# GpSimd stores odd partitions of dV and dK of pair 0, SyncE the even ones; dV of pair 3 in one store

## The chip, the cores and the metric

The kernel runs on one core of one Trainium2 chip. The metric is device time in microseconds (us) of one execution of the whole program. The core has five engines with instruction queues of their own: TensorE (PE), VectorE (DVE), ScalarE (ACT), GpSimd (POOL) and SyncE (SP), and sixteen DMA engines that move data between HBM and the on-chip memory (SBUF, 128 partitions). A store or load ("a DMA") is issued by one of the queues, cut into packets, and shared among the DMA engines; when all of them are done, a semaphore tells it.

## The reference

Attention with one query per head, forward and backward: 32 heads, 8192 keys and values per head, 128 numbers each, all in bf16.

```python
B, H, Sq, Skv, Dh = 1, 32, 1, 8192, 128
scores = jnp.einsum('bhqd,bhkd->bhqk', q, k) * Dh ** -0.5
attn = softmax(scores)
out = jnp.einsum('bhqk,bhkd->bhqd', attn, v)
# and the gradients of out with respect to q, k, v for a given grad_out
```

The outputs are out, dq, dk and dv. K and V (67 MB each) are read, dK and dV (67 MB each) are written. Each row of dV is the row's attention weight times grad_out, and each row of dK is the row's score gradient times q: outer products.

## The kernel before

**Pairs.** The 32 heads are taken as 16 pairs. Keys and values of one pair are 16384 rows of 128 numbers. A tile holds them as [128 partitions, 128 rows, 128 numbers]: a partition has 128 consecutive rows, 32 KB, and a tile is 4 MB. `rows_of(x, j)` gives the same arrangement in HBM.

**Buffers.** There are three buffers for K and two for V. The gradients are written in place: `outer(j, which, r)` overwrites an eighth of the K or V tile of pair j with an eighth of dK or dV, by one product on the DVE (line 291). When it has done the last piece of a store, the store is issued (lines 296 to 306). A K buffer can be loaded again when the dK that stood in it has been stored, so the K load of pair 3 waits for the stores of dK of pair 0, and the V load of pair 2 for the stores of dV of pair 0.

**Order.** The order of instructions is written out by hand. For each pair: scores from K on the PE, after DVE transposes; softmax; the products with V; dV (eight pieces); then, in the next pair's turn, dK (eight pieces). For pairs 0 and 1 dK is made in one stretch before the next pair's scores. `load_v(j + 1)` is issued after dK of pair j - 1, `load_k(j + 2)` after dV of pair j. SyncE issues nearly all loads and stores, in program order, and waits at each for what it overwrites or needs. `ENDS` says after which eighths a store is issued: by default two halves for pairs under `SPLIT` = 4, one whole store after that, and other pieces for the last pair.

**Pair 0.** dV of pair 0 has a way of its own (lines 296 to 301). Its first half (64 of each partition's 128 rows, 16 KB a partition, 2 MB together) is stored by GpSimd as soon as four of the eight products are done; its second half by SyncE after the eighth. dK of pair 0 goes by the default, two halves from SyncE.

**How GpSimd's bytes are dealt out.** A store that SyncE issues for 128 partitions puts the same bytes on all sixteen DMA engines. For a store that GpSimd issues for n partitions the kernel's arithmetic takes it that k engines are used, k being the largest divisor of n up to 16, starting at a place that moves on by k with every request; `cursor` keeps count of that place. `turn_to(engine)` moves it on to a wanted engine with a tiny load of a few bytes into a tile that nothing reads (`turned`); `share_out` then stores the partitions `first`, `first + 3`, `first + 6`, ... of one entry of `SHARES`. So each entry `(engine, first, n)` says on which engines n partitions go: for example n = 39 goes to 13 engines, three partitions on each. The seven entries together are all 128 partitions, in unequal parts: engine 4 gets none, engines 0, 1, 2 and 15 get twelve each. With `max_dma_last_dim=8192` a partition's 16 KB go as two packets of 8 KB.

**Waits of GpSimd.** The requests of GpSimd take turns among eight semaphores, so each waits until the request eight before it has landed.

Of the kernel before, what the change touches and what calls it, by code (L numbers as in the profile page):

```python
# [11 lines left out]
BF16 = mybir.dt.bfloat16  # L12
# [2 lines left out]

XK_BUFS = 3
EARLY = 3
ENDS = {("dk", 15): (2, 4, 8), ("dv", 15): (4, 8)}
SPLIT = 4
CH = 16  # L20
TB = 4
# [3 lines left out]
QD = 32  # L25
LOADS = {("k", 0): 4, ("v", 0): 4, ("v", 1): 4, ("k", 2): 2}
SHARED = 64
SHARES = ((5, 2, 7), (6, 0, 39), (6, 1, 39), (15, 23, 25), (10, 98, 10), (5, 117, 4), (5, 118, 4))
GP = 4


# [1 line left out]
def kernel(  # L33
# [11 lines left out]
    nc = tc.nc  # L45
    P = 128
# [14 lines left out]
    consts = ctx.enter_context(tc.tile_pool(name="consts", bufs=1))  # L61
# [14 lines left out]
    def rows_of(x, j, c=0, parts=1):  # L76
        L = NT // parts
        return x[0, 2 * j:2 * j + 2].rearrange("b s d -> (b s) d").rearrange("(p n) d -> p n d", p=P)[:, c * L:(c + 1) * L, :]

    def slots(X, c, parts):  # L80
        L = NT // parts
        return X[:, c * L:(c + 1) * L, :]
# [19 lines left out]
    load_v(1)  # L102
    load_k(2)

    turned = consts.tile([17, len(SHARES), 2, 2], BF16)
    cursor = [0, 0]

    def turn_to(engine):
        n = (engine - cursor[0]) % 16
        if n:  # L110
            rows = n if n > 1 else 17
            nc.gpsimd.dma_start(turned[0:rows, cursor[1]],
                                k[0, 0].rearrange("(p n) d -> p n d", p=P)[0:rows, 0:2, 0:2])
            cursor[1] += 1
        cursor[0] = engine

    def share_out(dst, src):
        for engine, first, n in SHARES:
            turn_to(engine)
            last = first + 3 * n - 2  # L120
            nc.gpsimd.dma_start(dst[first:last:3], src[first:last:3], max_dma_last_dim=8192)
            cursor[0] = (cursor[0] + max(i for i in range(1, 17) if n % i == 0)) % 16

    ident = consts.tile([P, P], BF16)
# [162 lines left out]
    def outer(j, which, r):  # L287
        x = st[j]
        G, dst = (Kt[j], out_2) if which == "dk" else (Vt[j], out_3)
        rep, row = x["ds"] if which == "dk" else x["p"], qd[j][:, 0 if which == "dk" else 1, :]  # L290
        nc.vector.tensor_tensor(  # L291
            slots(G, r, NU).rearrange("p n (a b) -> p n a b", b=R),
            slots(rep, r, NU).unsqueeze(2).to_broadcast([P, CH, D // R, R]),
            row.rearrange("p (a b) -> p a b", b=R).unsqueeze(1).to_broadcast([P, CH, D // R, R]),
            op=ALU.mult)
        if (which, j) == ("dv", 0):
            if (r + 1) * CH == SHARED:
                share_out(rows_of(dst, 0)[:, 0:SHARED, :], G[:, 0:SHARED, :])
            elif r == NU - 1:
                nc.sync.dma_start(rows_of(dst, 0)[:, SHARED:NT, :], G[:, SHARED:NT, :])  # L300
            return
        ends = ENDS.get((which, j), (4, 8) if j < SPLIT else (8,))
        if r + 1 in ends:
            i = ends.index(r + 1)
            a, b = (ends[i - 1] if i else 0) * CH, (r + 1) * CH
            nc.sync.dma_start(rows_of(dst, j)[:, a:b, :], G[:, a:b, :])
# [49 lines left out]
    for j in range(HP + 1):  # L356
# [30 lines left out]
        if j == 0:  # L387
            blocks(1)
            first = psT.tile([P, 512], F32, tag="T", name="first")
# [9 lines left out]
        if ends and j > 0:  # L399
            gather_copy(p_, "ds")  # L400
            if early:
                half(j, 0)
            for r in range(NU):
                if j == HP and r == NU - 2:
                    result(o_all, out_0)
                    gather(p_, "ds", st[p_]["m"])
                    result(dq_all, out_1)
                outer(p_, "dk", r)
            if j + 1 < HP:
                load_v(j + 1)  # L410
# [7 lines left out]
        if not ends:  # L418
            gather_copy(p_, "ds")
            outer(p_, "dk", 0)  # L420
            outer(p_, "dk", 1)
# [104 lines left out]
```

## Time and profile before

| what | value |
|---|---|
| time, median of 3 runs | 632.86 us (632.41 to 633.36) |
| time of the profiled execution | 633.73 us |
| its span, first to last instruction | 631.9 us |
| bytes moved by DMA | 268.98 MB, 426 GB/s on average |
| SyncE's queue, GpSimd's queue (share of 16 engines) | 98.5%, 0.8% |
| GpSimd's stores of dV of pair 0: first and last issue | 31.06 us, 46.70 us |
| their median time from issue to landing, by size | 6.7 to 19.9 us |
| SyncE issues the second half of dV of pair 0 | 37.67 us |
| SyncE issues dK of pair 0, two halves | from 47.25 us |
| V load of pair 2, K load of pair 3 issued | 65.57 us, 77.33 us |
| SyncE issues the last store (half of dK of pair 15) | 621.92 us |

The page cuts the span into 40 slices of 15.8 us. Its DMA row gives the mean busy share of the sixteen DMA engines in tenths (9 is 90% or more). "q1 hardware_dynamic" is SyncE's queue, "q0 software_dynamic" GpSimd's, "q8 instruction" fetches instructions. In the list of issues, SPq and POOL are SyncE and GpSimd; the first number is the start in us, the second how long the issue took, and brackets give the time the engine had waited before, and for what. Line numbers are those of the kernel before; in the changed kernel the same lines stand three to four lower.

### The profile page before, as it was taken

What the parts mean: (1) busy time and instruction counts of PE and PEld (TensorE: products, weight loads), DVE (VectorE), ACT (ScalarE), POOL (GpSimd) and SP (SyncE); (2) the same over time, 40 slices, a digit from 0 to 9 for tenths busy, and PEclk for the clock granted to TensorE, in tenths of its full rate; (3) what the DMA queues carried; (4) which work ended last, traced back from release to release, by engine and by line L of the source; (5) the groups of instructions that cost most, each with busy time, mean ns of one, the idle gap of its engine ahead of it and who ended that gap; (6) DMA issues with size and microseconds to landing.
All of it is one profiled execution on the core that took longest, in us unless ns stands there. A gap on an engine that the chain in (4) does not pass through costs nothing.

```text
span 631.9 us, 8032 instructions
## 1 busy us (share of the span) xinstructions
PE 470.0 (74%) x3256; PEld 250.0 (40%) x3256; DVE 517.0 (82%) x654; ACT 205.4 (32%) x460; POOL 11.6 (2%) x23
## 2 busy tenths in 40 slices
PE   4787868878787877776887767857679876797671
PEld 1443444254443525334363432624436343252440
DVE  6589897989879898796978969879697986988873
ACT  2441434043341605234052330603415133160331
POOL 2040000000000000000000000000000000000000
PEclk9989787778798887779878798877887778887685
DMA  8999999999999999999999999999999999999997
GB/s 363 435 399 425 437 432 422 430 433 436 431 429 435 433 430 430 430 434 431 430 429 432 431 432 430 430 425 432 432 430 432 431 432 429 431 431 435 427 421 324
DMA packets 13140, 268.98 MB, mean 426 GB/s; under 512 B 2096, under 2 KB 2096, under 8 KB 2096
## 3 DMA queue, kind: packets, MB, share of 16 engines
q1 hardware_dynamic: 12192, 266.36, 98.5%
q0 software_dynamic: 816, 2.10, 0.8%
q8 instruction: 25, 0.41, 0.2%
q14 instruction: 11, 0.09, 0.0%
q10 hardware_dynamic: 96, 0.02, 0.0%
HBM read 134.23 MB, written 134.23 MB: 425 GB/s over the span
## 4 chain that ended last, share of the span: by engine, by line
DMA 54%; PE 30%; DVE 11%; ACT 3%; issue 1%; DVEq 0%; SPq 0%; ACTq 0%
DMA Vt<-in_v_dram 22%; DMA out_dram<-Vt 14%; PE T_ps L216 12%; DMA Kt<-in_k_dram 10%; PE s_ps L199 9%; DMA out_dram<-Kt 8%; DVE Kt L291 3%; PE acc_p L266 3%; DVE Vt L291 2%; DVE XK_sb L189 2%; PE acc_ds L266 2%; ACT XV_sb L221 2%; PE dp_ps L233 2%; PE m_ps L283 1%; DVE sT L206 1%
## 5 line engine op out<-in xcount | busy, mean ns | idle before, releaser
L199 PE MATMUL s_ps<-XK_sb,q_win 128*128 128x512 bf16 x512 | 156.7, 445 | 58.2 <-DVE XK_sb L189 53.6
L291 DVE TENSOR_TENSOR Vt<-p_rep,qd 128x2048 bf16<-128x2048 bf16 x128 | 154.5, 1223 | 43.2 <-PE acc_p L266 32.9
L189 DVE STREAM_TRANSPOSE XK_sb<-Kt 128x1024 f32<-128x1024 f32 x128 | 150.4, 1218 | 33.3 <-DMA Kt<-in_k_dram 29.5
L216 PE MATMUL T_ps<-ident_f,Vt 128*128 128x128 f32 x1024 | 171.0, 321 | 8.6 <-DMA Vt<-in_v_dram 8.6
L221 ACT COPY XV_sb<-T_ps 128x512 f32<-128x512 f32 x256 | 140.3, 589 | 90.9 <-PE T_ps L216 90.2
L216 PEld LDWEIGHTS T_ps<-ident_f,Vt 128*128 128x128 f32 x1024 | 136.8, 165 | 47.0 <-issue 23.7
L291 DVE TENSOR_TENSOR Kt<-ds_rep,qd 128x2048 bf16<-128x2048 bf16 x128 | 149.5, 1214 | 3.0 <-PE acc_ds L266 2.5
L199 PEld LDWEIGHTS <-q_win 128*128 128x128 bf16 x512 | 52.5, 112 | 149.2 <-issue 119.0
L266 PE MATMUL acc_p<-Vt,win 128*32 128x512 bf16 x512 | 57.7, 455 | 3.2 <-ACT win L256 3.2
L441 ACT ACTIVATE e<-sT,nbias 128x128 f32<-128x128 f32 x16 | 8.2, 516 | 149.1 <-DVE nbias L437 149.1
L266 PEld LDWEIGHTS <-win 128*32 128x32 bf16 x1024 | 22.8, 99 | 61.3 <-issue 49.9
L266 PE MATMUL acc_ds<-Kt,win 128*32 128x512 bf16 x512 | 41.2, 415 | 4.6 <-ACT win L256 4.6
L233 PE MATMUL dp_ps<-XV_sb,do_win 128*32 128x512 bf16 x512 | 34.1, 382 | 13.4 <-ACT XV_sb L221 13.4
L256 ACT COPY win<-ds 64x128 bf16<-64x128 bf16 x32 | 9.5, 296 | 99.1 <-DVE ds L328 98.9
L233 PEld LDWEIGHTS <-do_win 128*32 128x32 bf16 x512 | 14.3, 94 | 29.0 <-issue 22.4
L442 PE MATMUL m_ps<-rs,ones_f 128*128 128x1 f32 x32 | 7.5, 305 | 24.4 <-ACT e L441 24.4
L428 PE MATMUL m_ps<-ident_f,top 128*128 128x128 f32 x16 | 4.8, 300 | 23.5 <-DVE top L426 23.5
L206 DVE STREAM_TRANSPOSE sT<-s_ps 128x512 f32<-128x512 f32 x16 | 11.5, 717 | 12.6 <-PE s_ps L199 12.6
L442 PEld LDWEIGHTS m_ps<-rs,ones_f 128*128 128x128 f32 x32 | 6.2, 241 | 27.6 <-ACT e L441 27.6
L453 ACT ACTIVATE p_rep<-e,rinv 128x512 bf16<-128x512 f32 x16 | 11.5, 722 | 13.3 <-DVE rinv L451 13.3
L428 PEld LDWEIGHTS m_ps<-ident_f,top 128*128 128x128 f32 x16 | 2.1, 133 | 31.0 <-issue 25.4
L185 ACT COPY do_win<-do_cols 64x4 bf16<-64x4 bf16 x32 | 6.6, 206 | 16.1 <-PE dp_ps L233 15.8
(59 smaller groups left out, 155.6 us busy)
## 6 DMA issues: line engine op xcount, KB each, us to landing
Kt<-in_k_dram SPq DMA_DIRECT2D x14, 4096.0 KB, 29.0
Vt<-in_v_dram SPq DMA_DIRECT2D x14, 4096.0 KB, 29.0
out_dram<-Vt SPq DMA_DIRECT2D x11, 4096.0 KB, 31.9
out_dram<-Kt SPq DMA_DIRECT2D x11, 4096.0 KB, 24.7
out_dram<-Vt SPq DMA_DIRECT2D x9, 2048.0 KB, 21.5
out_dram<-Kt SPq DMA_DIRECT2D x9, 2048.0 KB, 20.1
Vt<-in_v_dram SPq DMA_DIRECT2D x8, 1024.0 KB, 22.9
Kt<-in_k_dram SPq DMA_DIRECT2D x4, 1024.0 KB, 8.1
```

Of the source, the lines that this page charges most:

```text
L189: nc.vector.transpose(XK[j, u][:].rearrange("p g w i -> p (g w i)"), slots(Kt[j], u, NU).rearrange("p g d -> p (g d)").bitcast(F32))
L199: nc.tensor.matmul(st[j]["s"][:], lhsT=q_win[:, c, at:at + P], rhs=cols[:, c // 2, c % 2], start=(u == 0 and c == 0), stop=(u == NU - 1 an ...
L206: nc.vector.transpose(sT[:].rearrange("p g r -> p (g r)"), x["s"][:])
L216: nc.tensor.transpose(T_ps[:, i, :], words[:, m * P:(m + 1) * P], ident_f[:])
L221: nc.scalar.copy(XV[j][:, b * TB:(b + 1) * TB, :], st[j].pop(("T", c))[:])
L233: nc.tensor.matmul(out[b * QD:(b + 1) * QD, :], lhsT=do_win[:, b // 2, e2, at:at + QD], rhs=cols[:, z, e2, :, b * QD:(b + 1) * QD], start= ...
L256: nc.scalar.copy(win[t * M:(t + 1) * M, :, at:at + 4], src[t * M:(t + 1) * M])
L266: nc.tensor.matmul(acc[which][b * QD:(b + 1) * QD, :], lhsT=win[:, g, at:at + QD], rhs=X[:, 4 * g:4 * g + 4, :].rearrange("p n d -> p (n d)"),
L291: nc.vector.tensor_tensor(slots(G, r, NU).rearrange("p n (a b) -> p n a b", b=R), slots(rep, r, NU).unsqueeze(2).to_broadcast([P, CH, D // ...
L441: nc.scalar.activation(e[:].rearrange("p (u g) -> p u g", u=NU), x["sn"], ACT.Exp, bias=nbias[:], scale=scale, accum_out=rs[:])
L442: nc.tensor.matmul(x["m"][:, 0:1], lhsT=ones_f[:], rhs=rs[:], start=True, stop=True, skip_group_check=True)
L453: nc.scalar.activation(x["p"][:], e[:].unsqueeze(2).to_broadcast([P, NT, R]), ACT.Copy, scale=rinv[:])
```

## The change

Three things.

- The first half of dK of pair 0 now goes the way of the first half of dV: `share_out` is called for both.
- In both, GpSimd stores the odd partitions only, in six pieces each, by two new lists; the pieces take every fourth partition instead of every third. SyncE stores the even partitions, in one store of 64 partitions, 1 MB. The second halves are stored by SyncE whole, as dV's was.
- dV of pair 3 is stored whole after its eighth product instead of in two halves.

GpSimd thus issues twelve stores instead of seven, and twelve turning loads instead of seven; its bytes stay at 2.10 MB.

```diff
-ENDS = {("dk", 15): (2, 4, 8), ("dv", 15): (4, 8)}
+ENDS = {("dk", 15): (2, 4, 8), ("dv", 15): (4, 8), ("dv", 3): (8,)}
-SHARES = ((5, 2, 7), (6, 0, 39), (6, 1, 39), (15, 23, 25), (10, 98, 10), (5, 117, 4), (5, 118, 4))
+SHARES = {
+    "dv": ((5, 15, 4), (6, 25, 26), (15, 31, 25), (6, 3, 3), (7, 1, 2), (5, 9, 4)),
+    "dk": ((0, 119, 3), (5, 23, 14), (7, 25, 26), (7, 79, 10), (5, 1, 6), (7, 3, 5)),
+}
-    turned = consts.tile([17, len(SHARES), 2, 2], BF16)
+    turned = consts.tile([17, len(SHARES["dv"] + SHARES["dk"]), 2, 2], BF16)
-    def share_out(dst, src):
-        for engine, first, n in SHARES:
+    def share_out(which, dst, src):
+        for engine, first, n in SHARES[which]:
             turn_to(engine)
-            last = first + 3 * n - 2
-            nc.gpsimd.dma_start(dst[first:last:3], src[first:last:3], max_dma_last_dim=8192)
+            last = first + 4 * n - 3
+            nc.gpsimd.dma_start(dst[first:last:4], src[first:last:4], max_dma_last_dim=8192)
             cursor[0] = (cursor[0] + max(i for i in range(1, 17) if n % i == 0)) % 16
-        if (which, j) == ("dv", 0):
+        if j == 0:
             if (r + 1) * CH == SHARED:
-                share_out(rows_of(dst, 0)[:, 0:SHARED, :], G[:, 0:SHARED, :])
+                share_out(which, rows_of(dst, 0)[:, 0:SHARED, :], G[:, 0:SHARED, :])
+                nc.sync.dma_start(rows_of(dst, 0)[0:P:2, 0:SHARED, :], G[0:P:2, 0:SHARED, :])
             elif r == NU - 1:
                 nc.sync.dma_start(rows_of(dst, 0)[:, SHARED:NT, :], G[:, SHARED:NT, :])
             return
```

## The prediction

> **What bounds the kernel now.** I read the page first, parts 2 and 3: is any resource full over the whole span?
>
> ```profile
> span 631.9 us, 8032 instructions
> PE 470.0 (74%) x3256; PEld 250.0 (40%) x3256; DVE 517.0 (82%) x654; ACT 205.4 (32%) x460; POOL 11.6 (2%) x23
> ...
> DMA  8999999999999999999999999999999999999997
> ...
> q1 hardware_dynamic: 12192, 266.36, 98.5%
> q0 software_dynamic: 816, 2.10, 0.8%
> ```
>
> The 16 DMA engines are full from the first slice to the last: SyncE's queue (q1) and GpSimd's (q0) take 99.3% of them. No compute engine passes 82%. The bytes don't change, so the time can move only by what a DMA engine loses (waiting, slowed packets) and by how unevenly the 16 finish. Second view, the stretches around the end and around GpSimd's burst (columns: stretch, its length, busy us of PE, PEld, DVE, ACT, POOL, clock, DMA share, GB/s):
>
> ```profile
> 626.00:627.50 1.50, 0.00 (x0) 0.00 (x0) 0.00 (x0) 0.00 (x0) 0.00 (x0) 0.50 0.92 393
> 627.50:628.50 1.00, 0.00 (x0) 0.00 (x0) 0.00 (x0) 0.00 (x0) 0.00 (x0) 0.50 0.58 246
> 628.50:629.50 1.00, 0.00 (x0) 0.00 (x0) 0.00 (x0) 0.00 (x0) 0.00 (x0) 0.50 0.19 82
> 629.50:630.50 1.00, 0.00 (x0) 0.00 (x0) 0.00 (x0) 0.00 (x0) 0.00 (x0) 0.50 0.04 16
> ...
> 32.00:38.00 6.00, 5.42 (x56) 3.34 (x56) 5.26 (x5) 4.07 (x9) 3.81 (x7) 1.00 1.00 362
> 38.00:46.00 8.00, 5.50 (x43) 2.23 (x43) 6.41 (x13) 0.87 (x4) 2.72 (x4) 0.79 1.02 426
> ```
>
> From 627.5 the engines drop out one by one; the last one works alone near 630.5. That tail is what another division of GpSimd's bytes can change. In 32 to 38 us, while GpSimd's first requests start, every engine is slowed: 362 GB/s against 426. Third view, the times at which SyncE and GpSimd issue:
>
> ```profile
> 65.57 0.34 SPq L94 DMA_DIRECT2D Vt<-in_v_dram  x1
> 72.29 4.87 SPq L306 DMA_DIRECT2D out_dram<-Vt  x2
> 77.33 0.49 SPq L88 DMA_DIRECT2D Kt<-in_k_dram  x1
> 85.41 4.87 SPq L306 DMA_DIRECT2D out_dram<-Kt  x2
> ...
> 38.03 0.56 POOL L121 DMA_DIRECT2D out_dram<-Vt  x1 [2.23 <-DMA out_dram<-Vt]
> 42.42 0.60 POOL L121 DMA_DIRECT2D out_dram<-Vt  x1 [2.75 <-DMA out_dram<-Vt]
> 46.70 0.59 POOL L121 DMA_DIRECT2D out_dram<-Vt  x1 [3.07 <-DMA out_dram<-Vt]
> ```
>
> GpSimd is already held by landings: each request waits for the one eight back. The V load of pair 2 leaves at 65.57 because it overwrites the V of pair 0.
>
> **The sixteen engines.** The trace's DMA packets carry start, duration and size but no engine. On one engine a packet starts 3 to 4 ns before the one ahead of it ends, so they can be chained into 16. The 8 KB packets of GpSimd on each chain come out at 24 four times, 18 three times, 16 twice, 14 four times, 12, 6 and 0 (two chains are confused by one packet): just what the arithmetic of `turn_to` and `share_out` gives to engines (0,1,2,15), (6,7,8), (10,11), (9,12,13,14), 3, 5 and 4. So I can name engines, and count the new lists the same way. One row is 16 KB, two packets of 0.306 us. Rows by engine, and the end of its last packet in us:
>
> - 0, 1, 15: 12 rows, now 12, 11, 11; ends 627.7 to 628.0
> - 2: 12, now 11; 629.44
> - 3: 6, now 7; 628.28. 5: 3, now 4; 627.76
> - 4: 0, now 0; 629.28
> - 6: 9, now 7; 630.67. 7 and 8: 9, now 12; 627.7
> - 9: 7, now 8; 629.64. 10: 8, now 8; 628.83
> - 11: 8, now 7; 628.92. 12, 13, 14: 7, now 6; 628.2 to 628.6
>
> Two things explain ends that don't follow the rows. Engine 4 is slow by itself: its 32 KB packets take up to 1.29 us instead of 1.213, some 8.8 us over the run, so it needs the lead that its missing rows give. And the 16 KB instruction fetches (25 on the page's q8, about 0.95 us, and some 0.5 us more of slowed data) go in turn to eight engines: those with 14, 16, 16, 14, 14, 14 and 6 packets (9 to 14, then 5) and one of 6, 7, 8, which is the one that ends last. I take it for engine 6, the next after 5.
>
> **The change, part by part.**
>
> *Rows moved.* Engine 6 loses two: 630.67 - 2 x 0.61 = 629.46. Engines 7 and 8 gain three: 627.7 + 1.83 = 629.5; they had stood idle 0.8 us for the last store (issued 621.92), so perhaps 628.7. Engine 9 gains one: 630.25. Engine 2: 628.83; the others stay below 629.
>
> *Even partitions on SyncE.* For dV and for dK 64 rows, 4 on each engine, 2.43 us each. GpSimd's 2.10 MB stay 2.10 MB. SyncE issues a 1 MB store of dV at about 31.1 and loses 1 MB of dK at 47.25, so its queue is the same up to the end of dK of pair 0, but the second half of dV now stands 2.43 us further back. It landed last at 64.61, on an engine that had 24 packets of GpSimd before it (7.3 us). Now that engine has had 14 for dV and perhaps 4 of dK by then (5.5 us): 2.43 - 1.83 = 0.6 later at least, 2.4 if it has had 24 again. Following the two rings packet by packet, one of GpSimd's for each of SyncE's, I get 1.6. The V load of pair 2 would thus leave at 67.2 instead of 65.57. Queued behind it on SyncE is the first store of dV of pair 1, at 72.29, which isn't reached; who waits is engine 4, first to run out. Its first packet of that load took 2.03 us where 1.21 is usual, so it already lost 0.81; it arrives no later than before, and each us of delay is lost to it. Engine 4: 629.28 + 1.6 = 630.9 (629.9 to 631.7).
>
> *GpSimd's longer chain.* Twelve stores and twelve turning requests instead of seven and seven. The six of dK start at 47.25, when the DVE has done the first half, and pass through two rounds of waiting for the request eight back. Before, such a request landed 17.3 to 20.3 us after issue; the same walk through the rings puts the last landing at 77 to 83. The K load of pair 3, which overwrites K of pair 0, now waits for it; it left at 77.33. It costs nothing while it leaves before about 87: the engines still have the stores of dV of pair 1, which engine 4 ended at 87.6 and the mean engine at 92.1, and the lead that a load needs was 2.4 us (65.57 to 69.17 less one packet). Behind it on SyncE stands a store at 85.41. If that cover is gone, engine 4 pays each us in full.
>
> A lag can add to this: GpSimd's first packets came 3.8 us after the issue at 31.06, while the DVE's products of line 291 ran (from 32.36), and the same products run from 42.59 to 51.76, over the first dK requests. If each of the two rounds lags so, the last landing is near 87, which is why rival 1 below gets more than a tenth. The Trainium skill's page "DMA: Bandwidth & Descriptors", section "SWDGE vs HWDGE vs iDMA", says as much against this place: GpSimd writes its descriptors into SBUF, and the DVE's two-port mode locks it out meanwhile. By that rule the K load leaves at 87 and the time is rival 1's lower end; without it, the walk's 77 to 83 and my sum stand.
>
> *The burst.* At 362 instead of 428 GB/s (2 to 30 us), the 6 us lost 0.93 us on every engine. The four first stores held 110 rows; now 58. If the loss follows rows it falls by 0.44; if it follows requests, by nothing; a second burst with dK could at most repeat it (+0.93), but single requests at 38 to 47 us ran at 426. I take -0.2. Ten more requests of some three tiny packets (6 ns each) add up to 0.2. Together nothing.
>
> *dV of pair 3 whole.* The first half was issued at 140.84; at 147.8 SyncE's queue still held the V load that landed at 161.7, so a whole store is not late, and the V load behind it waits for the second half's end in both. Cover gone, it would cost a store's lead, 2.4 us. One completion less: nothing.
>
> **Sum.** The last packet of the profiled execution was engine 6's at 630.67 (span 631.9, time 633.73). After: engine 4 at 630.9, +0.2. But this execution is 0.87 above the median 632.86, and engine 6 met one packet at 392.9 us that took 0.63 too long; without it the last would have been at 630.0, and the change +0.9. I take +0.65: **633.5 us**. The wait at engine 6 goes; engine 4, and 9 behind it, are late next.
>
> **The rivals.**
> 1. *The dK chain holds the K load* (the side of slower). If the dK requests land 25 us after issue, since V's 32 KB packets double each turn of the ring, the last comes near 90, the load leaves at 90.5 instead of 77.33, and engine 4 loses 3.5 us more: 632.86 + 0.65 + 3.5 = 637; at 88.5 it is 635. It decides from 87. For it: GpSimd's waits above; against: the walk. 22%.
> 2. *The V load isn't later*, or engine 4 gets its wait back. Then engine 9 (630.25, less up to 0.44) is last against 630.67, and engines 6, 7, 8 at 629.5: 0.4 to 1.5 gained, 631.5. 22%.
> 3. *The late engine isn't 6 but 7 or 8.* It gains three rows: 632.5, +1.8, 634.7. Against: the order of the fetches. 8%.
>
> **How the numbers follow.** My own case has 45%, from 632.4 to 634.4 by its bounds (engine 4's 629.9 to 631.7, the executions' own 0.5). Something unseen: 3%, slower. 0.2%, 1.27 us, is about what a measurement of this kernel can tell from no change. Faster than 631.6: 0.15 of rival 2 and 0.03 of mine, 0.18. Within: 0.33 of mine and 0.07 of rival 2, 0.40. Slower than 634.1: 0.09 of mine, 0.22, 0.08, 0.03: 0.42. The range, 631.2 to 635.6, leaves out the far ends of rivals 1 and 2, some 0.2.
>
> **What would show it.** The V load of pair 2 at 66.2 to 68 us (right), at 65.6 or earlier (rival 2); the K load of pair 3 at 77.3 to 84 (right), past 87 (rival 1); six GpSimd stores from line 124 before 43 us, six from 47; the DMA share between 628.5 and 630.5 still over 0.1 on average, and 32 to 38 us at 360 to 400 GB/s. I am wrong if the tail ends before 629.5 or the engines run empty after 77 us.

## The result, and the profile after

The changed kernel takes **637.13 us** (median of 6 runs, 636.52 to 638.32); the kernel before, beside it, 633.0 us (6 runs, 632.41 to 634.14). The ratio is 1.0063, with a 95% interval of 1.0052 to 1.0074: slower by 0.6%, 4.1 us. The forecast was 633.5 us, with a range of 631.2 to 635.6.

The profiled execution of the changed kernel took 636.52 us, 0.6 us below its median, where that of the kernel before was 0.7 us above its own. So the two traces lie only 2.8 us apart, and the other 1.3 us is between executions of one kernel.

The page of the changed kernel, parts 2 and 3:

```profile
span 634.8 us, 8048 instructions
...
DMA  8999999999999999999999999999999999999997
GB/s 362 433 403 420 394 417 426 430 435 435 435 422 440 429 429 430 433 434 428 433 436 431 426 425 435 433 427 428 431 430 426 436 428 431 434 431 433 430 417 316
...
q1 hardware_dynamic: 12064, 266.36, 98.3%
q0 software_dynamic: 1152, 2.10, 0.9%
```

The DMA engines are as full as before. The loss isn't idle time: the fifth and sixth slices of 15.8 us (63 to 95 us) show 394 and 417 GB/s, where every later one up to the last two is at 422 to 440. The engines are busy and move less. The same in stretches (columns as in the prediction), first the changed kernel:

```profile
32.00:38.00 6.00, 4.57 (x50) 2.71 (x48) 5.61 (x6) 3.63 (x8) 3.73 (x7) 1.00 0.98 373
...
62.00:70.00 8.00, 5.86 (x42) 2.61 (x40) 6.80 (x10) 4.60 (x11) 0.00 (x0) 0.62 1.03 411
70.00:78.00 8.00, 7.12 (x54) 3.94 (x54) 7.34 (x13) 2.57 (x7) 0.00 (x0) 0.95 1.02 379
78.00:86.00 8.00, 1.91 (x32) 0.77 (x32) 7.21 (x9) 0.59 (x2) 0.00 (x0) 0.90 0.95 387
86.00:100.00 14.00, 11.35 (x68) 7.88 (x68) 9.45 (x10) 4.40 (x8) 0.00 (x0) 0.81 1.01 434
62.00:86.00 24.00, 14.89 (x127) 7.32 (x124) 21.36 (x30) 7.75 (x19) 0.00 (x0) 0.83 1.00 392
```

and the kernel before:

```profile
62.00:70.00 8.00, 5.42 (x41) 3.05 (x41) 6.80 (x11) 4.02 (x10) 0.00 (x0) 0.74 1.03 435
70.00:78.00 8.00, 7.61 (x57) 4.11 (x56) 7.90 (x11) 3.25 (x7) 0.00 (x0) 0.83 1.04 446
78.00:86.00 8.00, 3.53 (x46) 2.18 (x45) 6.38 (x9) 0.81 (x3) 0.00 (x0) 1.00 0.95 408
...
62.00:86.00 24.00, 16.55 (x140) 9.34 (x141) 21.07 (x30) 8.07 (x20) 0.00 (x0) 0.86 1.01 430
```

From 62 to 86 us the sixteen engines move 392 GB/s instead of 430, with the DMA share at 1.00. Over 24 us that is 24 x (1 - 392/430) = 2.1 us of work. From 86 us on both kernels run at full rate.

The packet records say which packets are slow. I add up what packets of 8, 16 and 32 KB took beyond their usual 0.309, 0.611 and 1.213 us, as a mean per engine. Between 62 and 90 us that is 0.12 us before and **2.00 us** after; over the whole run it is 3.89 and 5.80 us, so nearly all of the difference is made there. Of the 2.00 us, 1.34 belong to the eight 32 KB packets of each engine that load V of pair 2, above all those at its beginning (up to 1.47 us too long) and towards its end; the rest to the stores just before. The slow packets come at the same times on many engines (74 to 77.6 us and 80.3 to 84.3 us), and go on after the last 8 KB packet of GpSimd has ended at 70.8 us.

The loss is paid at the end. The tail of the changed kernel:

```profile
627.50:628.50 1.00, 0.00 (x0) 0.00 (x0) 0.00 (x0) 0.00 (x0) 0.00 (x0) 0.50 1.06 452
628.50:629.50 1.00, 0.00 (x0) 0.00 (x0) 0.00 (x0) 0.00 (x0) 0.00 (x0) 0.50 1.08 460
629.50:630.50 1.00, 0.00 (x0) 0.00 (x0) 0.00 (x0) 0.00 (x0) 0.00 (x0) 0.50 0.58 246
630.50:631.50 1.00, 0.00 (x0) 0.00 (x0) 0.00 (x0) 0.00 (x0) 0.00 (x0) 0.50 0.35 147
631.50:632.50 1.00, 0.00 (x0) 0.00 (x0) 0.00 (x0) 0.00 (x0) 0.00 (x0) 0.50 0.12 49
632.50:633.50 1.00, 0.00 (x0) 0.00 (x0) 0.00 (x0) 0.00 (x0) 0.00 (x0) 0.50 0.08 33
```

From 628.5 to 629.5 us all engines still work (DMA share 1.08), where before the share was 0.19. The mean engine ends at 630.98 instead of 628.57 us, the last at 633.52 instead of 630.67. The mean engine is already 2.2 us late at the end of the V load of pair 3 (its sixteen landings come at 123.61 instead of 121.46 us in the mean), so what comes later adds next to nothing. The issues of SyncE and GpSimd:

```profile
67.72 0.34 SPq L97 DMA_DIRECT2D Vt<-in_v_dram  x1
71.39 4.87 SPq L310 DMA_DIRECT2D out_dram<-Vt  x2
76.56 0.34 SPq L91 DMA_DIRECT2D Kt<-in_k_dram  x1
...
40.10 0.80 POOL L124 DMA_DIRECT2D out_dram<-Vt  x1 [1.85 <-DMA out_dram<-Vt]
...
46.63 0.57 POOL L124 DMA_DIRECT2D out_dram<-Kt  x1 [5.16 <-DVE Kt L294]
...
59.16 0.56 POOL L124 DMA_DIRECT2D out_dram<-Kt  x1 [1.31 <-DMA out_dram<-Kt]
```

The V load of pair 2 leaves at 67.72 us (before 65.57), the K load of pair 3 at 76.56 us, not held by GpSimd's dK, whose last store had landed at 72.75 us.

### The profile page after: what moved, and what is told of

Its sections match the earlier page's. It is cut to its first block, busy times and chain, and to the rows that moved or that the text cites. A ratio compares the mean times of both kernels' runs of the same rounds, so it can differ in the third digit from the quotient of the medians.

```text
span 634.8 us, 8048 instructions
## 1 busy us (share of the span) xinstructions
PE 459.4 (72%) x3256; PEld 246.7 (39%) x3256; DVE 516.3 (81%) x654; ACT 205.9 (32%) x460; POOL 17.0 (3%) x33
## 4 chain that ended last, share of the span: by engine, by line
DMA 57%; PE 24%; DVE 12%; ACT 3%; issue 2%; DVEq 0%; ACTq 0%; SPq 0%
DMA Vt<-in_v_dram 35%; DMA out_dram<-Vt 21%; PE T_ps L219 14%; PE s_ps L202 4%; PE acc_p L269 4%; DVE Kt L294 3%; DVE XK_sb L192 3%; DVE Vt L294 3%; ACT XV_sb L224 2%; PE dp_ps L236 2%; PE acc_ds L269 1%; DMA Kt<-in_k_dram 1%; ACT win L259 1%; DVE sT L209 1%; ACT p_rep L457 0%
## 5 line engine op out<-in xcount | busy, mean ns | idle before, releaser
L202 PE MATMUL s_ps<-XK_sb,q_win 128*128 128x512 bf16 x512 | 152.0, 433 | 66.3 <-DVE XK_sb L192 61.5
L219 PE MATMUL T_ps<-ident_f,Vt 128*128 128x128 f32 x1024 | 169.0, 319 | 13.0 <-DMA Vt<-in_v_dram 13.0
L219 PEld LDWEIGHTS T_ps<-ident_f,Vt 128*128 128x128 f32 x1024 | 135.4, 164 | 49.9 <-issue 24.2
L269 PE MATMUL acc_p<-Vt,win 128*32 128x512 bf16 x512 | 55.9, 439 | 3.4 <-ACT win L259 3.4
L322 PEld LDWEIGHTS m_ps<-pd,ones_f 128*128 128x128 f32 x32 | 8.7, 285 | 8.2 <-DVE prod L252 7.2
```

The source lines that it names most:

```text
L202: nc.tensor.matmul(st[j]["s"][:], lhsT=q_win[:, c, at:at + P], rhs=cols[:, c // 2, c % 2], start=(u == 0 and c == 0), stop=(u == NU - 1 an ...
L219: nc.tensor.transpose(T_ps[:, i, :], words[:, m * P:(m + 1) * P], ident_f[:])
L269: nc.tensor.matmul(acc[which][b * QD:(b + 1) * QD, :], lhsT=win[:, g, at:at + QD], rhs=X[:, 4 * g:4 * g + 4, :].rearrange("p n d -> p (n d)"),
L322: nc.tensor.matmul(x["m"][:, 1:3], lhsT=ones_f[:], rhs=x["pd"][:], start=True, stop=True, skip_group_check=True)
```

## The experiments

Each run is compared with the kernel before on the same chip. "The stretch" below is 62 to 86 us; a run has either 427 to 433 GB/s there and at most 0.41 us of slow packets, or 363 to 409 GB/s and 1.2 to 3.8 us. The table gathers what the following paragraphs find; "dK's first half" counts the store transfers in which it leaves, by SyncE and by GpSimd.

| run | dK's first half: SyncE + GpSimd | stretch, GB/s | slow packets 62 to 90, us per engine | ratio to before |
|---|---|---|---|---|
| before | 1 + 0 | 430 | 0.12 | 1 |
| changed | 1 + 6 | 392 | 2.00 | 1.0063 |
| e1 dV of pair 3 in halves | 1 + 6 | 387 | 2.27 | 1.0058 |
| e2 dV alone | 1 + 0 | 433 | 0.08 | 1.0028 |
| e3 dK alone | 1 + 6 | 398 | 1.60 | 1.0090 |
| e4 late V load | 2 + 0 | 428 | 0.27 | 1.0034 |
| e5 even and odd by SyncE | 2 + 0 | 432 | 0.09 | 1.0044 |
| e6 contiguous halves | 1 + 6 | 363 | 3.80 | 1.0112 |
| e7 requests without bytes | 2 + 0 | 430 | 0.09 | 1.0032 |
| e8 one request | 1 + 1 | 431 | 0.08 | 1.0033 |
| e9 one request, late | 1 + 1 | 430 | 0.11 | 1.0027 |
| e10 six requests, sooner | 1 + 6 | 392 | 1.94 | 1.0058 |
| e11 before, dealt out anew | 1 + 0 | 427 | 0.33 | 0.9998 |
| e12 lists exchanged | 1 + 6 | 395 | 1.48 | 1.0045 |
| e13 eight even requests | 1 + 8 | 395 | 1.95 | 1.0079 |
| e14 two requests | 1 + 2 | 409 | 1.23 | 1.0038 |
| e15 eight requests, late | 1 + 8 | 428 | 0.41 | 1.0135 |
| e16 dK's six requests alone | 1 + 6 | 397 | 1.71 | 1.0097 |
| e17 dV's twelve requests alone | 2 + 0 | 428 | 0.13 | 1.0075 |
| e18 one request, engine 4 spared | 2 + 1 | 402 | 1.63 | 1.0041 |

Where a run gives engine 4, the slow one, rows that the changed kernel spares it (e2, e5, e7 to e10, e13 to e17), that engine's end moves too, so the ratio alone decides nothing and the stretch does. In e2, for one, the slow engine, known by packets that take some 15 ns longer than the others', ends last, at 632.66 us instead of 629.28, with four rows more (4 x 0.61 = 2.4 us, and 0.9 besides that I haven't traced).

**Parts undone, first four runs.** I had three theories: the V load leaves too late, so that the engines come to it early and together (1); GpSimd's dK slows all engines (2); stores of every second partition are slow in themselves (3). The first run gives dV of pair 3 its two stores back:

```diff
-ENDS = {("dk", 15): (2, 4, 8), ("dv", 15): (4, 8), ("dv", 3): (8,)}
+ENDS = {("dk", 15): (2, 4, 8), ("dv", 15): (4, 8)}
```

> The changed kernel with dV of pair 3 stored in two halves again; all else of the change stays. In the changed kernel the DMA traffic runs at 411, 379 and 387 GB/s in 62 to 70, 70 to 78 and 78 to 86 us (before: 435, 446, 408), and the landings at 123 us are already 2.2 us late on average, of 2.4 at the end: dV of pair 3 comes later and should be worth nothing. Expected by every theory: 637 us, within 0.5 of the changed kernel. If the slow stretch at 62 to 86 us is not there this time and the time is still 637, it was an accident of one profile.

637.07 us (636.83 to 637.96), ratio 1.0058 (1.0043 to 1.0073), as the changed kernel. dV of pair 3 is worth nothing. The second run leaves dK as before, the third dV:

```diff
-        if j == 0:
+        if (which, j) == ("dv", 0):
```

> dV of pair 0 by the new division, dK of pair 0 in SyncE's two halves as before. SyncE's queue is 1 MB longer ahead of the V load of pair 2, which still leaves near 67 us. Theory 1 (the V load leaves too late for the engines, which come to it early and together): engines now come to it 2.4 us later than in the changed kernel, so none waits; 62 to 86 us at 425 GB/s or more; the time is then set by engine 4, whose lead over the others has shrunk by 4 rows (2.4 us): 633 to 635 us. Theory 2 (GpSimd's dK requests beside SyncE's stores slow all engines): also no slow stretch, since there are no dK requests. Theory 3 (stores of every second partition are slow in themselves): a slow stretch of about half, at 50 to 62 us where the even partitions of dV go out.

```diff
-    "dv": ((5, 15, 4), (6, 25, 26), (15, 31, 25), (6, 3, 3), (7, 1, 2), (5, 9, 4)),
+    "dv": ((5, 2, 7), (6, 0, 39), (6, 1, 39), (15, 23, 25), (10, 98, 10), (5, 117, 4), (5, 118, 4)),
...
+            step = 3 if which == "dv" else 4
...
+                if which == "dk":
                     nc.sync.dma_start(rows_of(dst, 0)[0:P:2, 0:SHARED, :], G[0:P:2, 0:SHARED, :])
```

> dV of pair 0 by the old seven pieces, all 128 partitions from GpSimd, and dK of pair 0 by the new division. SyncE's queue ahead of the V load of pair 2 is 1 MB shorter than in either kernel, so engines reach the load 2.4 us earlier, while the load still leaves at 65.6 us. Theory 1: more waiting than in the changed kernel, first packets of the load 1 to 4 us long, 639 us or more. Theory 2: GpSimd has 3.1 MB, its dK requests are queued behind those of dV and last until 85 us or later; slow stretch as in the changed kernel or longer, 637 to 640 us, with the stores slowed as well as the loads. Theory 3: half of the cost, 635 us.

The stretch of the second run (stretch, length, busy time of five engines, clock, DMA share, GB/s):

```profile
62.00:86.00 24.00, 15.80 (x143) 8.70 (x142) 21.36 (x30) 8.55 (x21) 0.00 (x0) 0.92 1.01 433
```

and of the third, with its K load of pair 3 from the list of issues:

```profile
62.00:86.00 24.00, 15.70 (x131) 8.37 (x131) 21.00 (x29) 7.85 (x19) 3.27 (x6) 0.86 1.00 398
...
90.83 0.34 SPq L91 DMA_DIRECT2D Kt<-in_k_dram  x1
```

dV alone: 635.79 us (634.44 to 635.88), ratio 1.0028 (1.0015 to 1.0041), no slow stretch. dK alone: 639.2 us (637.23 to 641.57), ratio 1.0090 (1.0059 to 1.0122), a slow stretch, and on top of it a K load held to 90.83 us, since GpSimd has both the old dV and the new dK to deal out; its slow engine ends at 636.22 us. The loss comes with dK. The fourth run makes the V load late without any other change: the last quarter of dV of pair 0 is stored behind the first quarter of dK in the kernel before.

```diff
+ENDS = {("dk", 15): (2, 4, 8), ("dv", 15): (4, 8), ("dk", 0): (2, 4, 8)}
...
-                nc.sync.dma_start(rows_of(dst, 0)[:, SHARED:NT, :], G[:, SHARED:NT, :])
+                nc.sync.dma_start(rows_of(dst, 0)[:, SHARED:96, :], G[:, SHARED:96, :])
...
+            if (which, j, i) == ("dk", 0, 0):
+                nc.sync.dma_start(rows_of(out_3, 0)[:, 96:NT, :], Vt[0][:, 96:NT, :])
```

> The kernel before, with the last quarter of dV of pair 0 (1 MB) stored behind the first quarter of dK of pair 0 instead of ahead of it, so that the V load of pair 2 leaves some 2.4 us later, near 68 us, as in the changed kernel; GpSimd's requests, the engines' bytes and their order up to the load are the same else. Theory 1: the slow loads of the changed kernel appear (62 to 86 us at 390 to 410 GB/s), 635.5 to 637 us. Theory 2 and 3: only engine 4 and 5 wait, no slow stretch (425 GB/s or more), engine 4 ends 2.4 us later: 634 to 635 us.

```profile
67.83 0.34 SPq L94 DMA_DIRECT2D Vt<-in_v_dram  x1
...
62.00:86.00 24.00, 15.30 (x133) 7.80 (x132) 21.36 (x30) 7.76 (x19) 0.00 (x0) 0.84 1.01 428
```

635.73 us (635.09 to 636.35), ratio 1.0034 (1.0021 to 1.0048). The load leaves at 67.83 us, as late as in the changed kernel, and the stretch stays at 428. So theory 1 falls as the cause of the slow stretch. The lateness has its own price: the slow engine ends at 631.56 instead of 629.28 us, 2.3 us for a load 2.26 us later.

**What of dK's sharing it is.** Four runs take it apart: SyncE stores even and odd partitions itself; GpSimd gets a contiguous half; GpSimd issues twelve requests without bytes; GpSimd's share goes in one request.

```diff
+                if which == "dk":
+                    nc.sync.dma_start(rows_of(dst, 0)[1:P:2, 0:SHARED, :], G[1:P:2, 0:SHARED, :])
+                else:
                     share_out(which, rows_of(dst, 0)[:, 0:SHARED, :], G[:, 0:SHARED, :])
```

> The changed kernel, with the odd partitions of the first half of dK of pair 0 stored by SyncE too, in a store of its own; GpSimd stores only its share of dV. Theory A (GpSimd's dK requests beside SyncE's stores slow all engines): 425 to 440 GB/s over 62 to 86 us, where the changed kernel has about 392. Theory B (a store of every second partition is slow in itself): 385 to 405 GB/s there. The time is that of the dV part alone in both, since engine 4 now stores four rows of dK: 635 to 636.5 by A, about 638 by B.

```diff
+            step = 4 if which == "dv" else 2
+            first = first if which == "dv" else P // 2 + first // 2
...
+                own = slice(0, P, 2) if which == "dv" else slice(0, P // 2)
+                nc.sync.dma_start(rows_of(dst, 0)[own, 0:SHARED, :], G[own, 0:SHARED, :])
```

> The changed kernel, with dK of pair 0 divided in the middle instead of by even and odd: SyncE stores partitions 0 to 63 of the first half, GpSimd 64 to 127, in the same six pieces on the same engines. Theory A (GpSimd's requests): 385 to 405 GB/s over 62 to 86 us, 636.5 to 638 us. Theory B (the alternation): 425 to 440 GB/s, 634 to 635.5 us.

```diff
+                if which == "dk":
+                    for i in range(12):
+                        nc.gpsimd.dma_start(turned[0:16, len(SHARES["dv"]) + i], k[0, 0].rearrange("(p n) d -> p n d", p=P)[0:16, 0:2, 0:2])
+                    nc.sync.dma_start(rows_of(dst, 0)[1:P:2, 0:SHARED, :], G[1:P:2, 0:SHARED, :])
+                else:
                     share_out(which, rows_of(dst, 0)[:, 0:SHARED, :], G[:, 0:SHARED, :])
```

> As the run before last (SyncE stores both the even and the odd partitions of dK), and GpSimd issues twelve requests of sixteen packets of 8 bytes at the time of dK in place of its stores: its requests without its bytes. If the number of GpSimd's requests slows the engines: 385 to 405 GB/s over 62 to 86 us and about 638 us. If it is the stores' bytes: 425 to 440 GB/s and 635 to 636.5 us, as without the twelve.

```diff
+                if which == "dk":
+                    nc.gpsimd.dma_start(rows_of(dst, 0)[1:P:2, 0:SHARED, :], G[1:P:2, 0:SHARED, :], max_dma_last_dim=8192)
+                else:
                     share_out(which, rows_of(dst, 0)[:, 0:SHARED, :], G[:, 0:SHARED, :])
```

> The changed kernel, with GpSimd's share of dK in one request of 64 rows, four on each engine, instead of six pieces and six turning requests: its bytes without the requests. If the bytes from GpSimd's queue slow the engines: 385 to 405 GB/s over 62 to 86 us and about 638 us (engine 4 has four rows more than in the changed kernel). If it is the number of requests: 425 to 440 GB/s and 635 to 636.5 us.

The contiguous half:

```profile
62.00:70.00 8.00, 5.54 (x57) 3.63 (x57) 7.02 (x10) 5.02 (x12) 0.00 (x0) 1.00 0.99 315
...
62.00:86.00 24.00, 14.69 (x131) 7.44 (x131) 21.36 (x29) 7.76 (x19) 0.00 (x0) 0.93 1.00 363
```

The one request:

```profile
67.04 0.34 SPq L97 DMA_DIRECT2D Vt<-in_v_dram  x1
...
62.00:86.00 24.00, 17.36 (x147) 10.04 (x147) 21.01 (x31) 8.88 (x22) 0.00 (x0) 0.86 1.01 431
```

Times: e5 636.16 us (635.93 to 636.31), e6 640.62 (639.82 to 640.68), e7 635.51 (634.94 to 635.87), e8 635.53 (634.8 to 635.97); ratios in the table. The alternation of partitions is not the cause: it alone costs nothing (e5), and without it the loss is larger (e6). This settles theory 3. The requests without bytes cost nothing (e7), nor do the bytes in one request (e8, with the V load nearly as late as in the changed kernel, 67.04 us). Both halves of my theory 2, bytes or requests, fall as they stood; bytes in several requests are left, until the last run (e18) shows the loss with a single one.

**Late packets, or pieces?** Two runs ask whether stores of GpSimd that are still under way when the V load comes are the cause: one request, issued late beside the load; and the six pieces, issued sooner because dV takes two requests only.

```diff
+                if which == "dv":
                     share_out(which, rows_of(dst, 0)[:, 0:SHARED, :], G[:, 0:SHARED, :])
...
+        if (j, which, r) == (1, "dv", 0):
+            nc.gpsimd.dma_start(turned[0:16, len(SHARES["dv"])], G[0:16, 0:2, 0:2])
+            nc.gpsimd.dma_start(rows_of(out_2, 0)[1:P:2, 0:SHARED, :], Kt[0][1:P:2, 0:SHARED, :], max_dma_last_dim=8192)
```

> The changed kernel, with GpSimd's share of dK in one request of 64 rows, four on each engine, that is issued only after the first product of dV of pair 1 (about 66 us): evenly spread, but late, so that its packets lie beside the V load of pair 2. Theory C (what slows the engines is that stores of GpSimd's queue are still pending when the load comes, from about 62 to 77 us): 385 to 410 GB/s over 62 to 86 us. Theory D (it is the division into small uneven pieces): 425 to 440 GB/s. Time about 636 to 638.5 us by C, 635 to 636.5 us by D (engine 4 has four rows more than in the changed kernel).

```diff
-    "dv": ((5, 15, 4), (6, 25, 26), (15, 31, 25), (6, 3, 3), (7, 1, 2), (5, 9, 4)),
+    "dv": ((0, 1, 32), (0, 3, 32)),
```

> The changed kernel, with GpSimd's share of dV in two even requests of 32 rows instead of six pieces and six turning requests; dK in its six uneven pieces as before. The dK requests then meet the limit of eight only at the end and land some us sooner. Theory C (late stores beside the load): 410 to 435 GB/s over 62 to 86 us, the more the sooner the last landing. Theory D (uneven pieces): 385 to 405 GB/s, whenever they land. Time 635 to 636.5 us by C, 637 to 638.5 us by D (engine 4 has four rows more).

The late one request:

```profile
62.00:86.00 24.00, 16.85 (x151) 9.57 (x151) 21.35 (x30) 9.29 (x23) 1.16 (x2) 0.93 1.01 430
...
85.73 0.34 SPq L91 DMA_DIRECT2D Kt<-in_k_dram  x1
```

The six pieces, issued from 47.21 to 57.07 us:

```profile
62.00:86.00 24.00, 14.43 (x131) 7.31 (x131) 21.36 (x30) 7.76 (x19) 0.00 (x0) 0.92 1.00 392
```

Late stores don't slow the load: GpSimd's packets run from 75.3 to 84.7 us right beside it at 430 GB/s (635.13 us, 634.59 to 636.24). Six pieces do, sooner or not (637.45 us, 637.09 to 637.61). Theory C, lateness, falls. In e9 the K load of pair 3 leaves at 85.73 us, over 8 us later than in the kernel before, and the slow engine ends at 631.58 us all the same, not later than in e7 (631.91), where that load leaves at 76.59 us (the V load of pair 2 leaves at 64.93 us in both).

Beside these two, the kernel before was dealt out anew, to see whether the late engine is engine 6 as the prediction took it, and as the one candidate for a faster kernel:

```diff
-SHARES = ((5, 2, 7), (6, 0, 39), (6, 1, 39), (15, 23, 25), (10, 98, 10), (5, 117, 4), (5, 118, 4))
+SHARES = ((7, 2, 7), (6, 0, 39), (6, 1, 39), (15, 23, 25), (10, 98, 10), (5, 117, 4), (14, 118, 4))
```

> The kernel before, with two starting engines of GpSimd's pieces changed: the first piece of seven starts at engine 7 instead of 5, the last of four at 14 instead of 5. Engine 6, taken for the last one (630.67 us), loses two rows, 5 too, 7 and 8 one each; 12, 13, 15, 0 and 1 gain one each and 14 gains two. By the ends read from the trace before, engine 9 is then last at 629.64, 1.0 us sooner: ratio 0.9975 to 0.9995. If engine 6 was not the late one, the ratio is 0.9995 to 1.002.

633.42 us (632.87 to 634.7), ratio 0.9998 (0.9989 to 1.0007). The last landing in its trace is at 630.29 us instead of 630.67, and two engines share it. No run of this study beats the kernel before.

**Number or unevenness of the pieces.** The lists of dV and dK exchanged; eight even requests; two uneven ones.

```diff
-    "dv": ((5, 15, 4), (6, 25, 26), (15, 31, 25), (6, 3, 3), (7, 1, 2), (5, 9, 4)),
-    "dk": ((0, 119, 3), (5, 23, 14), (7, 25, 26), (7, 79, 10), (5, 1, 6), (7, 3, 5)),
+    "dv": ((0, 119, 3), (5, 23, 14), (7, 25, 26), (7, 79, 10), (5, 1, 6), (7, 3, 5)),
+    "dk": ((5, 15, 4), (6, 25, 26), (15, 31, 25), (6, 3, 3), (7, 1, 2), (5, 9, 4)),
```

> The changed kernel with the two lists of pieces exchanged: dV of pair 0 by dK's list, dK by dV's. If any six uneven pieces of dK slow the engines: 385 to 410 GB/s over 62 to 86 us, 636.5 to 638.5 us. If it is the particular list of dK: 425 to 440 GB/s there, and 633 to 635.5 us.

```diff
+                if which == "dk":
+                    for first, n, step in [(16 * i + 1, 8, 2) for i in range(8)]:
+                        last = first + step * (n - 1) + 1
+                        nc.gpsimd.dma_start(rows_of(dst, 0)[first:last:step, 0:SHARED, :], G[first:last:step, 0:SHARED, :], max_dma_last_dim=8192)
...
```

> The changed kernel, with GpSimd's share of dK in eight requests of eight rows, which follow each other round the engines (four rows on each in the end), without turning requests. If the number of GpSimd's store requests slows the engines: 385 to 410 GB/s over 62 to 86 us, 637 to 638.5 us. If it is the uneven spread: 425 to 440 GB/s, 635 to 636.5 us.

```diff
+                if which == "dk":
+                    for first, n, step in ((1, 40, 2), (81, 24, 2)):
...
```

> The changed kernel, with GpSimd's share of dK in two requests of 40 and 24 rows without turning requests: ten engines get four rows each, then the next twelve two each, so that six engines end with 6 rows, four with 4 and six with 2. If the uneven spread slows the engines: 385 to 415 GB/s over 62 to 86 us, 636.5 to 638.5 us. If it is the number of requests: 425 to 440 GB/s, 635 to 636.5 us.

Eight even requests:

```profile
62.00:86.00 24.00, 15.77 (x131) 8.37 (x131) 20.86 (x31) 7.86 (x19) 0.00 (x0) 0.86 1.00 395
```

Two uneven ones:

```profile
62.00:86.00 24.00, 15.48 (x131) 7.90 (x130) 21.36 (x30) 7.76 (x19) 0.00 (x0) 0.83 1.00 409
```

e12: 636.74 us (636.6 to 636.95), e13: 638.8 us (638.26 to 639.09), e14: 636.31 us (635.49 to 637.38). The particular list is not it (395 GB/s with the lists exchanged), and unevenness isn't needed (395 with eight even requests).

**Whose requests count.** Eight late requests; dK's six alone, with dV stored by SyncE; dV's twelve alone, with dK stored by SyncE.

```diff
+                if which == "dv":
                     share_out(which, rows_of(dst, 0)[:, 0:SHARED, :], G[:, 0:SHARED, :])
...
+        if (j, which, r) == (1, "dv", 0):
+            nc.gpsimd.dma_start(turned[0:16, len(SHARES["dv"])], G[0:16, 0:2, 0:2])
+            first = 1
+            for n in 8 * (8,):
+                nc.gpsimd.dma_start(rows_of(out_2, 0)[first:first + 2 * n - 1:2, 0:SHARED, :], Kt[0][first:first + 2 * n - 1:2, 0:SHARED, :], max_dma_last_dim=8192)
+                first += 2 * n
```

> The changed kernel, with GpSimd's share of dK in eight even requests of eight rows that are issued only after the first product of dV of pair 1, beside the V load of pair 2; the run with one request at this place had 430 GB/s over 62 to 86 us. If several store requests slow what runs while and after they land: below 415 GB/s over 70 to 94 us, 637 to 639 us. If only requests between the stores of dK do: 425 to 440 GB/s, 635 to 636.5 us.

```diff
+                if which == "dv":
+                    nc.sync.dma_start(rows_of(dst, 0)[1:P:2, 0:SHARED, :], G[1:P:2, 0:SHARED, :])
+                else:
+                    first = 1
+                    for n in (16, 16, 8, 8, 8, 8):
+                        nc.gpsimd.dma_start(rows_of(dst, 0)[first:first + 2 * n - 1:2, 0:SHARED, :], G[first:first + 2 * n - 1:2, 0:SHARED, :], max_dma_last_dim=8192)
+                        first += 2 * n
```

> The changed kernel, with the odd partitions of dV stored by SyncE (a store of its own) and GpSimd's share of dK in six even requests (16, 16, 8, 8, 8 and 8 rows): six of its requests in all. If the requests of dK's stage count: 385 to 410 GB/s over 62 to 86 us, 637 to 638.5 us. If the number of both stages together counts, from eight on: 425 to 440 GB/s, 635 to 636.5 us.

```diff
+                if which == "dk":
+                    nc.sync.dma_start(rows_of(dst, 0)[1:P:2, 0:SHARED, :], G[1:P:2, 0:SHARED, :])
+                else:
+                    first = 1
+                    for n in 4 * (8,) + 8 * (4,):
+                        nc.gpsimd.dma_start(rows_of(dst, 0)[first:first + 2 * n - 1:2, 0:SHARED, :], G[first:first + 2 * n - 1:2, 0:SHARED, :], max_dma_last_dim=8192)
+                        first += 2 * n
```

> The changed kernel, with the odd partitions of dK stored by SyncE and GpSimd's share of dV in twelve even requests (four of 8 rows, eight of 4 rows), without turning requests. If the requests of dK's stage count: 425 to 440 GB/s over 62 to 86 us, 635 to 636.5 us. If the number of both stages together counts: 385 to 410 GB/s in the stretch that follows, 637 to 638.5 us.

dK's six alone:

```profile
54.00:62.00 8.00, 6.11 (x26) 2.27 (x25) 6.81 (x9) 0.00 (x0) 0.00 (x0) 1.00 1.01 371
...
62.00:86.00 24.00, 14.46 (x131) 7.24 (x130) 21.35 (x30) 7.76 (x19) 0.00 (x0) 0.92 0.99 397
```

dV's twelve alone:

```profile
62.00:86.00 24.00, 17.94 (x151) 10.41 (x151) 20.84 (x31) 9.31 (x23) 0.00 (x0) 0.86 1.00 428
```

The eight late ones:

```profile
62.00:86.00 24.00, 17.64 (x156) 10.08 (x157) 21.36 (x30) 9.97 (x24) 4.94 (x9) 0.93 1.01 428
...
94.00:100.00 6.00, 4.10 (x24) 2.27 (x22) 3.17 (x9) 1.19 (x4) 0.00 (x0) 0.99 0.71 262
100.00:108.00 8.00, 7.24 (x50) 4.01 (x50) 6.14 (x7) 4.66 (x11) 0.00 (x0) 0.58 0.97 358
```

e16: 640.09 us (638.74 to 640.61); e17: 638.54 us (638.21 to 638.74); e15: 642.54 us (641.47 to 642.76). The requests of dK's stage are enough by themselves, six in the whole kernel; dV's stage is harmless even with twelve. (In e16 the engines are slow from 54 us on, at 371 GB/s, which the table's 1.71 us leaves out. Engine 4 has eight rows more in both; e17's time is that engine's.) In e15 the V load, which runs beside the eight requests, is not slowed, but the loads of K and V that follow them from 95 us are: 1.89 us of slow packets per engine from 90 to 112 us, where the kernel before has 0.05. There the K load also leaves 8 us after the point from which it costs, which is most of e15's time.

**The prediction's other terms, with the loss taken out.** The last run was to show whether the number of GpSimd's dK requests is all that was missed: one request that leaves engine 4 out, the four partitions that are left stored by SyncE.

```diff
+                if which == "dv":
+                    share_out(which, rows_of(dst, 0)[:, 0:SHARED, :], G[:, 0:SHARED, :])
+                else:
+                    turn_to(5)
+                    nc.gpsimd.dma_start(rows_of(dst, 0)[1:120:2, 0:SHARED, :], G[1:120:2, 0:SHARED, :], max_dma_last_dim=8192)
+                    nc.sync.dma_start(rows_of(dst, 0)[121:P:2, 0:SHARED, :], G[121:P:2, 0:SHARED, :])
```

> The changed kernel, with GpSimd's share of dK in one request of 60 rows that starts at engine 5, so that fifteen engines get four rows each and engine 4 none; SyncE stores the four odd partitions that are left (121 to 127). If the number of dK's store requests is all that the prediction missed: 425 to 440 GB/s over 62 to 86 us, and its 633.5 us, 632.4 to 634.5, ratio 0.999 to 1.002. If something else in the changed kernel costs the 3.6 us that were missed: 636 to 638 us, ratio 1.004 to 1.008.

```profile
68.65 0.35 SPq L97 DMA_DIRECT2D Vt<-in_v_dram  x1
...
62.00:86.00 24.00, 14.72 (x131) 7.43 (x131) 21.28 (x32) 7.76 (x19) 0.00 (x0) 0.93 1.00 402
```

636.23 us (635.88 to 637.13), ratio 1.0041 (1.0027 to 1.0054): missed, and with it the theory as it stood. With a single store request of GpSimd for dK the slow stretch is there all the same (402 GB/s, 1.63 us); what sets this run apart from e8 (431) is a turning request, 60 partitions instead of 64, a second store of SyncE for the other four, and with them a V load that leaves at 68.65 instead of 67.04 us. So the run didn't show what it was made for, the sum without the loss; that wasn't reached in any run.

**What the runs leave.** In every run that has the loss, GpSimd stores part of dK's first half, and that half leaves in three or more store transfers; no run with fewer than three, or without GpSimd, has it (in e15, where the transfers come later, the slow packets do too). That describes twenty traces, one of each kernel; it was read off when all had been run, no run was made to test it, and it is no mechanism. The time at which the V load leaves was not held constant, but doesn't separate the runs by itself: it is 64.1 to 64.9 us in six of the runs without the slow stretch, but 67.04 in e8 and 67.83 in e4, and 65.69 in e3, 66.65 in e10 and 67.55 in e16, which have it. In e3 the load is as early as in the kernel before (65.57), and in e10 and e16 its first packet comes only 5 us after its issue, so that no engine was waiting for it. Shown is where the time goes (the stores from 62 us and above all the load that follows), and that it is none of these alone: the lateness of the load, bytes, requests, alternation, the particular list, unevenness, packets beside the load. Why dV's stage is free of it, and what slows a load after the stores have landed, stays open. The Trainium skill's page "DMA: Bandwidth & Descriptors", section "Latency and other measured facts", gives copies that lose rate when the rows of neighbouring partitions lie 512 KiB or more apart, and infers, unverified, that streams in lock-step then meet on the same HBM channels. Here the rows lie 32 KB apart, and no run moved an address to try that; the transfers from 86 us on, with the engines as far apart as in the slow load (the sixteen landings within 5.9 us in the K load of pair 3, 6.1 in the slow one), ran at 434 GB/s.

## Why the prediction was wrong

**The step that failed is "The burst".** It said of GpSimd's dK that "a second burst with dK could at most repeat it (+0.93), but single requests at 38 to 47 us ran at 426", and ended with "Together nothing". The packets between 62 and 90 us took 1.88 us per engine more than before (2.00 less 0.12), twice the bound, as a mean over the sixteen engines. Of the 2.41 us by which the mean engine ends later this is 1.9; the other 0.5 I haven't divided further. Two things went wrong in this step. Its bound came from the row that looked alike, GpSimd's requests of dV in the kernel before, but dV's stage is free of this loss even with twelve requests (e17), while dK's six alone have it (e16): a row from one place was no bound for the other. What makes the difference between the two places stays open. And it looked for the price while the requests run; most of it falls on the load that comes after.

**The rest, point by point.**

- *Full engines* (right). A loss on all engines reaches the end undiminished: 2.2 us at 123 us, 2.4 at the end.
- *V load later* (right). 67.72 us, forecast 67.2, within 66.2 to 68. The slow engine, known by its longer packets, ends at 631.57 us; forecast 630.9, bounds 629.9 to 631.7 (some of its time is slow packets too, so the fit is better than this step earned). e4 has the lateness alone and prices it at 2.3 us for 2.26 us, where I had 1.6 for 1.6.
- *Order at the end* (wrong). Engine 4 should have been last. Four others end after it, at 631.9, 632.1, 633.1 and 633.5 us, and all others should have been at 630.25 or before. In part this is the failed step again: a loss that comes to all engines lets those with little lead end behind the slow one, and the 2.41 us of the mean engine on top of 630.25 are 632.66. The last two lie 0.5 and 0.9 us beyond that, which I can't place; the trace doesn't name the engines.
- *K load not held, rival 1* (right in the result, the landing sooner than forecast: 72.75 us, where the walk gave 77 to 83). The cover to 87 us was about right: at 85.73 us the load cost nothing (e9), at 90.83 it did (e3, slow engine 7 us later with its slow stretch included), at 95.06 much (e15). The Trainium skill's page "DMA: Bandwidth & Descriptors", section "SWDGE vs HWDGE vs iDMA", says that the DVE in its two-port mode can lock GpSimd out of the memory into which GpSimd writes its descriptors. In the run where GpSimd has nothing else to do (e16) its first packet of dK came 4.0 us after the issue, in the changed kernel that of dV 3.8 us; a lag of this size is there, and no run shows what makes it, but it is not one that holds the load to 87 us.
- *Burst at 32 to 38 us* (right). 373 GB/s, within 360 to 400.
- *dV of pair 3* (right). Nothing: 637.07 with halves, 637.13 without.
- *Rivals 2 and 3*. Rival 2 falls with the V load. Rival 3 can't be told: e11 moved rows away from engine 6 and gained 0.4 us in the trace, forecast 1.0, and nothing in the median.
- *Sum*. Engine 4's +0.2 in the trace became +0.9 by the slow engine's own end (631.57 less 630.67, the last landing before) and +2.85 by the last one's. One sign came true for another reason: the DMA share from 628.5 to 630.5 us was over 0.1 (1.08 and 0.58) because all engines were late. No rival stood for a loss on all engines; the 3% for something unseen was all that was left for it.

## What to carry to other kernels

When all DMA engines are full over the whole span, read GB/s stretch by stretch beside the busy share: a loss can hide in packets that take longer, with every engine at 1.00. A price read from one place of a program (a second request stream during dV) needn't hold at another that looks the same (during dK); when an edit moves an operation to a place that the trace doesn't show, bound it by more than the nearest row, and give a loss on all engines a chance of its own. Splitting a store among two queues isn't free because its bytes are: here dK's half in one request from each queue kept the rate (e8), and in three or more with GpSimd among them it cost 1.2 to 3.8 us on each of the sixteen engines, in the mean.

## What the runs showed that I had not expected

- A load can be slow after GpSimd's stores have landed: in the changed kernel the last of them has landed at 72.75 us, and the V load loses 1.34 us per engine, most of it from 74 to 77.6 and from 80.3 to 84.3 us.
- GpSimd's stores in one request right beside that load don't slow it (430 GB/s with 128 packets of 8 KB between 75.3 and 84.7 us), nor do twelve store requests of dV.
- Storing every second partition costs nothing: even and odd partitions by SyncE run at 432 GB/s.
- One engine of the sixteen takes about 15 ns longer for a packet all through every run. When the V load left 2.26 us late with nothing else changed, that engine ended 2.3 us later.
